# Attention scores of two head pairs in one excursion of the matrix engine, and the values' product in halves around two second layers

## The chip, the cores and the metric

The kernel runs on one core of a Trainium2 chip. The time is that of the whole program on the device, in microseconds. Before the change it is 648.01 us, the median of three runs (647.19 to 648.02).

The core's engines are named as the profile names them: PE multiplies matrices (PEld is its loading of weights), DVE, ACT and POOL work on vectors, SP issues transfers. Each engine takes its instructions from its own queue, in order.

## The reference

Windowed attention over 4 batches, 8 heads, 768 positions and head size 64, with a gated two-layer network behind it (512 to 2048 to 512), all in float32:

```
scores = q @ k.T / sqrt(64) - slope[h] * dist        # 8 global keys, 96 local keys; the rest is masked
a = exp(scores - max);  a = a / (sum(a) + 1e-9)
x = (a @ v), heads side by side: 3072 x 512
h = x @ w_in
out = (h * clip(h + 3, 0, 6) / 6) @ w_out
```

## The kernel before

**Blocks.** The 3072 rows are 8 blocks of 384 rows (three tiles of 128). For the network, the 2048 hidden features are 16 slices of 128. Each slice has a first layer (`first`, L172: 12 matmuls of 384 columns into a PSUM bank of the pool `ps_h`, named hp, which has two banks) and a second layer (`second`, L204: 9 matmuls of 512 columns into the block's three accumulators). Numbers are split in a high and a low part so that two roundings make one float32; that is why each product is three matmuls. Between the layers stands the gate: relu on ACT (L183), a product on DVE (L184), the high part `gh` on POOL (L190) and the low part `gl` on DVE (L197). The tile `g` has one buffer, so the gate of the next slice starts when `gl` is made.

**Slices in pairs.** In the layers of blocks 2 to 7 (`twos`, L490) the slices go in pairs: two first layers, then two steps of other work, then the second layers of the pair before, then two more steps. So a block has 8 slice pairs and the steps 0 to 31: steps 4m and 4m+1 stand behind the first layers of pair m, 4m+2 and 4m+3 behind the second layers that follow them. `attention` (L713) fills these steps with the attention of the next block; each list of functions in `units` is one step.

**A head pair's late attention.** A block has four head pairs (`Pair`, pr 0 to 3, numbered n over all blocks).
- `scale` (L865, POOL) multiplies the queries in their loaded room, in place. There are three rooms; `load_next` (L320) loads pair n + 3 into pair n's room on SP's queue.
- `packed` (L867) makes the scores: 24 small matmuls (48 records in a trace, L879) on parts of the array of 64 rows by 32 columns, into the two banks s and t, one for each head of the pair. `weigh` (L900) then takes each of the three tiles and two heads: a reduction on DVE that also leaves the least value (L908), and the exponential on ACT (L912).
- `sum_up` (DVE) and `normalize` (L932, POOL, two instructions for each tile).
- `spread` (L954, DVE, two transposes for each tile) into the tile `blocks`, whose pool `bp` has one buffer.
- `send` (L960): four transfers on SP's queue copy `blocks` into the pair's rows of `weights_of`.

An interruption of the full-size matmuls of the layers by such small ones is called an excursion here. Before the change the scores of the four pairs stand at the steps 0, 5, 10 and 16 (`TURNS`), and the later functions 3, 4 and 5 steps behind them. The scaling of the next pair's queries stands in the step of the scores.

**The values.** `weighted` (L688) multiplies the four pairs' rows of `weights_of` with the values, on parts of 32 rows by 64 columns, into four banks: one of hp for pair 0, x, t and s for pairs 1, 2 and 3. It stops halfway (`yield`). Its first matmuls read all of `weights_of`. At its end `put_x` (L155) copies each bank into the block's input: high part on ACT (L158), low part on DVE (L159). Before the change the first half runs between the two second layers behind step 25, by the list `between`, and the second half in step 26; the pairs' matmuls of a chunk go in the order 3, 2, 1, 0.

**Order.** `in_order` (L665) keeps the queues of PE, SP and POOL in the order in which the program is written. The order on ACT and DVE is made by a planner that places an instruction where its inputs and buffers are there by its own reckoning.

**The stage before the layers.** `rest_of_third` (L675) attends for the rest of block 2 in the last 8 slices of block 1 and scales the first late pair of block 3. Blocks 3 to 7 attend in the layers of blocks 2 to 6, as described. Block 7's layers hold no attention.

Of the kernel before, what the change touches and what calls it, by code (L numbers as in the profile page):

```python
# [9 lines left out]
F32 = mybir.dt.float32  # L10
# [9 lines left out]
P = 128  # L20
NT = 3
TB = NT * P
NTB = S // TB
NPAIR = H // 2
NKT = DM // P
NF = DF // P
BANK = 512
# [14 lines left out]
PW = PREV + NG + GQ  # L42
# [4 lines left out]
PLAIN = -1 / np.sqrt(D)  # L47
EARLY = 9
ROOMS = 3
TURNS = (0, 5, 10, 16)  # L50
LEAD = 6
WAKE = 9
FIRST = 3
# [10 lines left out]
class Kernel:  # L64
# [425 lines left out]
    def twos(self, steps):  # L490

        for i in range(0, len(steps), 2):
            after = []
            for block, f, x, acc in steps[i:i + 2]:
                g = self.gate(self.first(f, x))
                gh = self.high(g, True)
                after.append((block, f, acc, gh, self.rest(g, gh)))
            yield
            yield
            for self.last in self.pending:  # L500
                self.finish()
                if self.between:
                    self.between.pop()()
            self.pending = after
            yield
            yield
# [30 lines left out]
    def banded(self, flag):  # L537
# [12 lines left out]
        with ExitStack() as early, ExitStack() as words:  # L550
            x0 = self.x_tiles(self.pool("x0", 1, ctx=early, side="right"))
            xs = [x0, self.x_tiles(), self.x_tiles()]
# [8 lines left out]
            with ExitStack() as ctx:  # L561
# [8 lines left out]
                pairs = [Pair(self, n, xs[n // NPAIR], True) for n in range(EARLY)]  # L570
# [6 lines left out]
                for n in range(-2, EARLY + 1):  # L577
# [5 lines left out]
                    if n + 2 < EARLY:  # L583
                        weigh = []
# [46 lines left out]
            for _ in self.halves(todo):  # L631
                pass
            self.decoded_to(2 * NF - 1)
        self.up = self.pool("up", 3, side="right")
        self.bp = self.pool("bp", 1, side="right")
        self.late_tiles()
        self.op = self.pool("op", 3, side="right")
# [1 line left out]
        units, pairs = self.rest_of_third(xs[2], NF - next_f[1])  # L639
# [1 line left out]
            for unit in units[k]:  # L641
                unit()
        self.finish()
        self.pending, self.between = [], []
        self.stage = "layers"
        x, ahead = xs[2], pairs[-1]
        for i in range(2, len(self.blocks)):
            units, x_next = [], None
            if i + 1 < len(self.blocks):
                x_next = self.x_tiles()  # L650
                units, ahead = self.attention(i + 1, x_next, ahead)
            else:
                units = [[]] * 4 + [[lambda: self.doubt(flag)]]
# [7 lines left out]
            x = x_next  # L661
# [13 lines left out]
    def rest_of_third(self, x, slices):  # L675

        units = [[] for _ in range(2 * NF)]
        pairs = [Pair(self, n, x, False) for n in range(EARLY, 3 * NPAIR + 1)]
        pairs[0].scale()
        for p, (me, after) in enumerate(zip(pairs, pairs[1:])):  # L680
            at = units[3 * p + 1:]
            at[0] += [me.packed, after.scale, lambda me=me: self.load_next(me.n, False)]
            at[1] += [me.sum_up] + [lambda t=t, me=me: me.normalize(t) for t in range(NT)]
            at[2] += [lambda t=t, me=me: me.spread(t) for t in range(NT)] + [me.send]
        units[2 * slices - 1].append(lambda: list(self.weighted(pairs[:-1])))
        return units, pairs

    def weighted(self, pairs):  # L688


        nc, block, tb = self.nc, pairs[0].n // NPAIR, pairs[0].tb
        out = {}
        for pair in pairs[::-1]:
            bank = self.bank("xts"[pair.pr - 1]) if pair.pr else self.ps_h.tile([P, BANK], F32, name="hp")
            out[pair.pr] = bank[:, 0:TB]
        groups = self.weights_of.rearrange("p j t g s q -> p j (t g) s q")
        chunks = [(CHUNKS, 0, NT * GROUPS, GROUPS)]
        for c in range(0 if tb else PREV // GQ, CHUNKS):
            chunks.append((c, max(0, c - PREV // GQ), min(NT * GROUPS, c + 1), (c + 1) % GROUPS))
        for n, (c, g0, g1, slot) in enumerate(chunks):  # L700
            if n == len(chunks) // 2:
                yield
            for pr in out:
                own = slice(32 * pr, 32 * pr + 32)
                for j in range(2):
                    nc.tensor.matmul(out[pr][j * D:(j + 1) * D, g0 * GQ:g1 * GQ], lhsT=self.values_of[own, c, j * D:(j + 1) * D],  # L706
                                     rhs=groups[own, j, g0:g1, slot], start=(c == CHUNKS), stop=(c == CHUNKS - 1),
                                     tile_position=(32 * pr, j * D))
        for pr in sorted(out):
            self.put_x(pairs[0].x, pr, out[pr])  # L710
        self.load_values(block + 1)

    def attention(self, i, x, first):  # L713

        units = [[] for _ in range(2 * NF - 2)]
        pairs = [first]
        first.x = x
        for p in range(NPAIR):
            n = i * NPAIR + p
            me, after = pairs[p], Pair(self, n + 1, x, False) if n + 1 < len(self.blocks) * NPAIR else None  # L720
            pairs.append(after)
            at = units[TURNS[p]:]
            at[0] += [me.packed] + [a.scale for a in (after,) if a] + [lambda me=me: self.load_next(me.n, False)]
            at[3] += [me.sum_up, lambda me=me: me.normalize(0), lambda me=me: me.normalize(1)]
            at[4] += [lambda me=me: me.normalize(2), lambda me=me: me.spread(0)]
            at[5] += [lambda me=me: me.spread(1), lambda me=me: me.spread(2), me.send]
        values = self.weighted(pairs[:NPAIR])
        units[25].append(lambda: self.between.append(lambda: next(values)))
        units[26].append(lambda: next(values, None))
        return units, pairs[NPAIR]  # L730


    def general_setup(self):
# [109 lines left out]
class Pair:  # L843
# [20 lines left out]
        _, q = kk.loaded(self.n)  # L864
        nc.gpsimd.tensor_scalar(out=q, in0=q, scalar1=kk.over[:, self.pr:self.pr + 1], scalar2=0.0, op0=ALU.mult, op1=ALU.add)  # L865

    def packed(self):  # L867


        nc, kk = self.nc, self.k  # L870
        self.sums = kk.up.tile([P, 2, 2 * NT], F32, name="sums")
        banks = [kk.bank(b)[:, 0:NT * PW].rearrange("p (t c) -> p t c", t=NT) for b in "st"]
        keys, queries = kk.loaded(self.n)
        for t in range(NT):
            for g in range(GROUPS):
                own, c = slice(g * GQ, (g + 1) * GQ), t * TG + g * GQ
                for j in range(2):
                    rows = slice(j * D, (j + 1) * D)
                    nc.tensor.matmul(banks[j][own, t], lhsT=queries[rows, t, own], rhs=keys[rows, c:c + PW], start=True, stop=True,  # L879
                                     tile_position=(j * D, g * GQ))  # L880
        for t in range(NT):
            self.weigh(t, [bank[:, t] for bank in banks], kk.up.tile([P, 2, PW], F32, name="n"), 0)

    def scores(self, t):
        nc, kk = self.nc, self.k
        if t == 0:
            self.sums = kk.up.tile([P, 2, 2 * NT], F32, name="sums")
        if t != 1:
            self.banks = [kk.bank("s")[:, 0:2 * W].rearrange("p (i c) -> p i c", i=2) for _ in range(2)]
        sp = [self.banks[j][:, t % 2] for j in range(2)]  # L890
        e = kk.up.tile([P, 2, W], F32, name="n")
        lo = self.low(t)
        c = slice(t * TG + lo, t * TG + W)
        keys, queries = kk.loaded(self.n)
        for j in range(2):
            rows = slice(j * D, (j + 1) * D)
            nc.tensor.matmul(sp[j][:, lo:W], lhsT=queries[rows, t], rhs=keys[rows, c], start=True, stop=True)  # L897
        return lambda: self.weigh(t, sp, e, lo)

    def weigh(self, t, sp, e, lo):  # L900
        nc, kk, end = self.nc, self.k, self.end
        for j in range(2):
            h, i = 2 * self.pr + j, 2 * t + j
            if self.plain:
                d, scale = (kk.p0 if lo else kk.p1)[:, h], PLAIN
            else:
                d, scale = kk.dl[:, 0 if self.first(t) else 1], SLOPES[h]
            nc.vector.tensor_tensor_reduce(out=e[:, j, lo:end], in0=sp[j][:, lo:end], in1=d, op0=ALU.add, op1=ALU.min, scale=scale,  # L908
                                           scalar=3.0e38, accum_out=self.least[:, i:i + 1])
        for j in range(2):  # L910
            i = 2 * t + j
            nc.scalar.activation(out=e[:, j, lo:end], in_=e[:, j, lo:end], func=AF.Exp, bias=self.least[:, i:i + 1], scale=-1.0,  # L912
                                 accum_out=self.sums[:, 0, i:i + 1])
        if self.n <= 2:
            kk.held = nc.cur_bb.bb.instructions[-1].name
        self.rows.append(e)

    def sum_up(self, t=None):

# [145 lines left out]
```

## Time and profile before

| | |
|---|---|
| median of three runs | 648.01 us |
| profiled execution, its time | 647.65 us |
| profiled execution, its span | 645.9 us |
| granted PE clock, mean | 0.999 |
| PE busy | 634.3 us (98%) |
| DVE busy | 354.9 us (55%) |
| ACT busy | 255.9 us (40%) |
| POOL busy | 167.4 us (26%) |
| excursions of scores in the layers of blocks 2 to 6 | 20, with 48 records each |

The profile shows one execution. A row of a timeline has the start and the duration in us, the engine, the line of the kernel, the operation, the tile written and those read, the shapes and the count; in square brackets stands how long the engine was idle before it, and what ended that. A row of the chain of waits has start, duration and what ran. Matmuls overlap: a row's duration is longer than the distance to the next row's start, and the distance is what PE's stream takes.

### The profile page before, as it was taken

To read this page: it belongs to the slowest core of one execution; us is meant where nothing else is said; L and a number is where in the kernel's file an instruction comes from. 1 tells how busy PE (TensorE), PEld (TensorE's weight loads), DVE (VectorE), ACT (ScalarE), POOL (GpSimd) and SP (SyncE) were. 2 spreads that over 40 slices of the span, in tenths; PEclk is the share of its full clock that TensorE was granted. 3 is DMA by queue.
4 is the path that set the end of the run, shared out by engine and by line. 5 is a ranking of instruction groups with operands and counts; after the bars stand their busy time and mean duration, and the time that the engine had idled before them with its cause. 6 is when DMAs were issued, how large, how long until landed. Compare 5 with 4: busy or idle time off the path is not lost.

```text
span 645.9 us, 14423 instructions
## 1 busy us (share of the span) xinstructions
PE 634.3 (98%) x5593; PEld 557.5 (86%) x5593; DVE 354.9 (55%) x1066; ACT 255.9 (40%) x706; POOL 167.4 (26%) x371
## 2 busy tenths in 40 slices
PE   9989999999999999999999999999999999999997
PEld 7768999888888888888888888888888888899985
DVE  5889999996645552455534564255623555222222
ACT  5897877775415321242223231143212522221111
POOL 4668000000422441124302332033311242012100
PEclk9999999999999999999999999999999999999999
DMA  7675554543334421242232241223312311110001
GB/s 280 173 227 178 161 159 135 159 135 126 96 73 144 100 79 31 71 123 70 60 98 75 63 102 48 67 79 86 92 31 69 106 33 31 33 50 1 1 1 54
DMA packets 34334, 59.78 MB, mean 93 GB/s; under 512 B 3280, under 2 KB 21200, under 8 KB 33488
## 3 DMA queue, kind: packets, MB, share of 16 engines
q1 hardware_dynamic: 33968, 58.50, 31.4%
q8 instruction: 46, 0.75, 0.5%
q14 instruction: 32, 0.26, 0.1%
q10 hardware_dynamic: 288, 0.26, 0.1%
HBM read 41.16 MB, written 6.29 MB: 73 GB/s over the span
## 4 chain that ended last, share of the span: by engine, by line
PE 89%; DVE 4%; ACT 3%; DMA 1%; POOL 1%; issue 1%; SPq 0%; POOLq 0%; ACTq 0%; DVEq 0%
PE hp L172 40%; PE acc L204 36%; PE sp L879 2%; DVE xl L159 2%; PE sp L204 2%; PE tp L204 1%; PE xp L204 1%; PE sp L706 1%; ACT n L912 1%; DMA wst<-w 1%; POOL n L932 1%; PE tp L706 1%; DMA load<-pairs 1%; PE xp L972 1%; PE sp L897 1%
## 5 line engine op out<-in xcount | busy, mean ns | idle before, releaser
L183 ACT ACTIVATE g<-hp,small 128x384 f32<-128x384 f32 x127 | 73.8, 581 | 261.3 <-PE hp L172 174.5
L172 PE MATMUL hp<-xh,w1h 128*128 128x384 f32 x512 | 174.2, 340 | 0.7 <-DVE xl L159 0.3
L172 PE MATMUL hp<-xh,w1l 128*128 128x384 f32 x512 | 172.4, 337 | 0.1
L172 PE MATMUL hp<-xl,w1h 128*128 128x384 f32 x512 | 171.7, 335 | 0.0
L190 POOL TENSOR_SCALAR gh<-g 128x384 fp32r<-128x384 f32 x104 | 53.5, 515 | 424.4 <-DVE g L184 397.6
L184 DVE SCALAR_TENSOR_TENSOR g<-g,hp 128x384 f32<-128x384 f32 x128 | 70.7, 552 | 122.0 <-ACT g L183 120.7
L204 PE MATMUL acc<-w2h,gh 128*128 128x512 f32 x336 | 133.2, 396 | 0.0
L204 PE MATMUL acc<-w2h,gl 128*128 128x512 f32 x336 | 131.9, 393 | 0.0
L204 PE MATMUL acc<-w2l,gh 128*128 128x512 f32 x336 | 131.7, 392 | 0.0
L197 DVE TENSOR_TENSOR gl<-g,gh 128x384 fp32r<-128x384 f32 x128 | 71.4, 558 | 66.4 <-POOL gh L190 59.0
L172 PEld LDWEIGHTS hp<-xh,w1h 128*128 128x128 f32 x512 | 96.1, 188 | 7.0 <-DVE xl L159 2.3
L912 ACT ACTIVATE n<-n,least 128x136 f32<-128x136 f32 (+2 forms) x192 | 79.9, 418 | 54.2 <-DVE least L908 53.4
L172 PEld LDWEIGHTS hp<-xl,w1h 128*128 128x128 f32 x512 | 96.1, 188 | 2.6
L172 PEld LDWEIGHTS hp<-xh,w1l 128*128 128x128 f32 x512 | 96.1, 188 | 0.9 <-DVE w1l L439 0.8
L932 POOL TENSOR_SCALAR n<-n,sums 128x136 f32<-128x136 f32 (+2 forms) x186 | 82.4, 460 | 39.7 <-DVE sums L923 23.8
L204 PEld LDWEIGHTS acc<-w2h,gh 128*128 128x128 f32 x336 | 63.1, 188 | 15.4 <-issue 3.8
L204 PEld LDWEIGHTS acc<-w2h,gl 128*128 128x128 f32 x336 | 63.0, 188 | 13.8 <-DVE gl L197 0.3
L204 PEld LDWEIGHTS acc<-w2l,gh 128*128 128x128 f32 x336 | 63.1, 188 | 11.3
L954 DVE STREAM_TRANSPOSE blocks<-n 128x256 f32<-128x256 f32 x138 | 51.2, 424 | 22.8 <-POOL n L932 21.4
L912 ACT ACTIVATION_READ_ACCUMULATOR n<-n,least 128x1 f32 x192 | 36.3, 189 | 0.0
L399 ACT ACTIVATE wz<-wst 128x512 f32<-128x512 f32 x32 | 21.6, 679 | 5.7 <-DVE w2l L439 3.9
L446 DVE CUSTOM_DVE_ANT_0 wz<-wz,we 128x1024 uint16<-128x1024 uint16 x32 | 22.2, 695 | 1.3 <-POOL we L404 0.9
(126 smaller groups left out, 728.6 us busy)
## 6 DMA issues: line engine op xcount, KB each, us to landing
wst<-w SPq DMA_DIRECT2D x32, 512.0 KB, 3.6
load<-pairs SPq DMA_DIRECT2D x31, 444.0 KB, 3.5
weights<-blocks SPq DMA_DIRECT2D x92, 120.0 KB, 2.4
values<-values SPq DMA_DIRECT2D x6, 1024.0 KB, 5.4
out<-o SPq DMA_DIRECT2D x23, 256.0 KB, 2.4
values<-pairs SPq DMA_DIRECT2D x9, 384.0 KB, 3.6
out<-o ACTq DMA_DIRECT2D x1, 256.0 KB, 3.0
load<-pairs SPq DMA_DIRECT2D x1, 252.0 KB
```

The lines of the kernel that those rows point to most:

```text
L159: nc.vector.tensor_tensor(out=xl[:, pair, :], in0=ps, in1=xh[:, pair, :].bitcast(F32), op=ALU.subtract)
L172: self.nc.tensor.matmul(hp, lhsT=self.w1(w, f)[:, kt, :], rhs=a[:, kt, :], start=(n == 0), stop=(n == 3 * NKT - 1))
L183: nc.scalar.activation(out=g, in_=hp, func=AF.Relu, bias=self.three, scale=1.0)
L184: nc.vector.scalar_tensor_tensor(out=g, in0=g, scalar=6.0, in1=hp, op0=ALU.min, op1=ALU.mult)
L190: self.nc.gpsimd.tensor_scalar(out=gh, in0=g, scalar1=1.0, scalar2=0.0, op0=ALU.mult, op1=ALU.add)
L197: self.nc.vector.tensor_tensor(out=gl, in0=g, in1=gh.bitcast(F32), op=ALU.subtract)
L204: self.nc.tensor.matmul(acc[tt], lhsT=a[:, tk], rhs=self.w2(w, f), start=(f == 0 and j == 0), stop=(f == NF - 1 and j == 2))
L399: self.nc.scalar.activation(out=self.z[i].bitcast(F32), in_=words[:, :, 1].bitcast(F32), func=AF.Abs)
L446: tt(out=z, in0=z, in1=self.e.pop(i), op=ALU.add)
L912: nc.scalar.activation(out=e[:, j, lo:end], in_=e[:, j, lo:end], func=AF.Exp, bias=self.least[:, i:i + 1], scale=-1.0, accum_out=self.sums ...
L932: nc.gpsimd.tensor_scalar(out=e[:, j, lo:end], in0=e[:, j, lo:end], scalar1=over, scalar2=0.0, op0=ALU.mult, op1=ALU.add)
L954: nc.vector.transpose(out=self.blocks[:, :, t, 4 * s:4 * s + 4], in_=e[:, :, c:c + P].rearrange("p j (b q) -> p j b q", b=4))
```

## The change

- The scores of two pairs of a block stand in one step, at the steps 2 and 14 (`TURNS`). The first pair of such a couple writes one bank of hp and the bank x, the second s and t. For the first pair, head 0 is weighed over all tiles before head 1.
- In a couple, the first pair's `sum_up`, `normalize`, `spread` and `send` stand 3, 4 and 5 steps behind the scores, the second pair's 5, 6 and 7.
- The queries of the next couple's first pair are scaled in the step of the scores, those of its second pair 5 steps later. In the stage before the layers, the second late pair of block 3 is scaled too.
- The pool `up`, which holds the scores' tiles, has 6 buffers instead of 3.
- The first half of the values runs in step 25, ahead of both second layers, the second half in step 26 as before; `between` is gone. The pairs' matmuls of a chunk go in the order 0, 1, 2, 3.

The diff, cut to its core:

```
-TURNS = (0, 5, 10, 16)
+TURNS = (2, 14)
...
                 self.finish()
-                if self.between:
-                    self.between.pop()()
...
-        self.up = self.pool("up", 3, side="right")
+        self.up = self.pool("up", 6, side="right")
...
-        x, ahead = xs[2], pairs[-1]
+        x, ahead = xs[2], pairs[-2:]
...
     def rest_of_third(self, x, slices):
-        pairs = [Pair(self, n, x, False) for n in range(EARLY, 3 * NPAIR + 1)]
+        pairs = [Pair(self, n, x, False) for n in range(EARLY, 3 * NPAIR + 2)]
         pairs[0].scale()
-        for p, (me, after) in enumerate(zip(pairs, pairs[1:])):
+        for p, (me, after) in enumerate(zip(pairs[:-2], pairs[1:])):
...
-        units[2 * slices - 1].append(lambda: list(self.weighted(pairs[:-1])))
+        at[4].append(pairs[-1].scale)
+        units[2 * slices - 1].append(lambda: list(self.weighted(pairs[:-2])))
...
     def weighted(self, pairs):
-        for pair in pairs[::-1]:
+        for pair in pairs:
...
-    def attention(self, i, x, first):
+    def attention(self, i, x, pairs):
         units = [[] for _ in range(2 * NF - 2)]
-        pairs = [first]
-        first.x = x
-        for p in range(NPAIR):
-            n = i * NPAIR + p
-            me, after = pairs[p], Pair(self, n + 1, x, False) if n + 1 < len(self.blocks) * NPAIR else None
-            pairs.append(after)
-            at = units[TURNS[p]:]
-            at[0] += [me.packed] + [a.scale for a in (after,) if a] + [lambda me=me: self.load_next(me.n, False)]
-            at[3] += [me.sum_up, lambda me=me: me.normalize(0), lambda me=me: me.normalize(1)]
-            at[4] += [lambda me=me: me.normalize(2), lambda me=me: me.spread(0)]
-            at[5] += [lambda me=me: me.spread(1), lambda me=me: me.spread(2), me.send]
+        for pair in pairs:
+            pair.x = x
+        pairs = pairs + [Pair(self, n, x, False) for n in range(i * NPAIR + 2, min(i * NPAIR + 6, len(self.blocks) * NPAIR))]
+        for p in range(0, NPAIR, 2):
+            couple, after = pairs[p:p + 2], pairs[p + 2:p + 4]
+            at = units[TURNS[p // 2]:]
+            at[0] += [lambda me=me, first=first: me.packed(first) for me, first in zip(couple, (True, False))]
+            at[0] += [a.scale for a in after[:1]] + [lambda me=me: self.load_next(me.n, False) for me in couple]
+            at[5] += [a.scale for a in after[1:]]
+            for k, me in enumerate(couple):
+                at[2 * k + 3] += [me.sum_up, lambda me=me: me.normalize(0), lambda me=me: me.normalize(1)]
+                at[2 * k + 4] += [lambda me=me: me.normalize(2), lambda me=me: me.spread(0)]
+                at[2 * k + 5] += [lambda me=me: me.spread(1), lambda me=me: me.spread(2), me.send]
         values = self.weighted(pairs[:NPAIR])
-        units[25].append(lambda: self.between.append(lambda: next(values)))
-        units[26].append(lambda: next(values, None))
-        return units, pairs[NPAIR]
+        for k in (25, 26):
+            units[k].append(lambda: next(values, None))
+        return units, pairs[NPAIR:]
...
-    def packed(self):
+    def packed(self, first=False):
-        banks = [kk.bank(b)[:, 0:NT * PW].rearrange("p (t c) -> p t c", t=NT) for b in "st"]
+        banks = [kk.ps_h.tile([P, BANK], F32, name="hp"), kk.bank("x")] if first else [kk.bank("s"), kk.bank("t")]
+        banks = [bank[:, 0:NT * PW].rearrange("p (t c) -> p t c", t=NT) for bank in banks]
...
-        for t in range(NT):
-            self.weigh(t, [bank[:, t] for bank in banks], kk.up.tile([P, 2, PW], F32, name="n"), 0)
+        self.rows = [kk.up.tile([P, 2, PW], F32, name="n") for _ in range(NT)]
+        for heads in ((0,), (1,)) if first else ((0, 1),):
+            for t in range(NT):
+                self.weigh(t, [bank[:, t] for bank in banks], self.rows[t], 0, heads)
...
-    def weigh(self, t, sp, e, lo):
+    def weigh(self, t, sp, e, lo, heads=(0, 1)):
-        for j in range(2):
+        for j in heads:
```

More of the change, by code (lines that the diff above doesn't have):

```diff
@@ L643, in banded @@
         self.finish()
-        self.pending, self.between = [], []
+        self.pending = []
         self.stage = "layers"
-        x, ahead = xs[2], pairs[-1]
+        x, ahead = xs[2], pairs[-2:]
         for i in range(2, len(self.blocks)):
@@ L897, in scores @@
             nc.tensor.matmul(sp[j][:, lo:W], lhsT=queries[rows, t], rhs=keys[rows, c], start=True, stop=True)
+        self.rows.append(e)
         return lambda: self.weigh(t, sp, e, lo)
-    def weigh(self, t, sp, e, lo):
+    def weigh(self, t, sp, e, lo, heads=(0, 1)):
         nc, kk, end = self.nc, self.k, self.end
-        for j in range(2):
+        for j in heads:
             h, i = 2 * self.pr + j, 2 * t + j
@@ L909, in weigh @@
                                            scalar=3.0e38, accum_out=self.least[:, i:i + 1])
-        for j in range(2):
+        for j in heads:
             i = 2 * t + j
@@ L915, in weigh @@
             kk.held = nc.cur_bb.bb.instructions[-1].name
-        self.rows.append(e)
     def sum_up(self, t=None):
```

## The prediction

> **What bounds the kernel now.** I read the page's shares first, then its chain of work that ended last, then the waits of the matrix engine, and last the timelines of single excursions and of the engines around them.
>
> ```profile
> PE 634.3 (98%) x5593; PEld 557.5 (86%) x5593; DVE 354.9 (55%) x1066; ACT 255.9 (40%) x706; POOL 167.4 (26%) x371
> ...
> PEclk9999999999999999999999999999999999999999
> ...
> PE 89%; DVE 4%; ACT 3%; DMA 1%; POOL 1%; issue 1%; SPq 0%; POOLq 0%; ACTq 0%; DVEq 0%
> ...
> PE hp L172 <- DVE xl L159: 0.3, 2, 0.2
> ```
>
> PE is busy 98% of the span and holds 89% of the chain; in the layers it hardly waits. A change gains by what it takes out of PE's queue and loses by any wait that it puts there. The other engines count only where their work comes late for PE.
>
> One excursion of scores, in PE's timeline (start, duration):
>
> ```profile
> 294.48 0.39 PE L204 MATMUL acc<-w2l,gh 128*128 128x512 f32 x1
> 294.70 0.39 PE L204 MATMUL acc<-w2h,gl 128*128 128x512 f32 x1
> 295.02 0.30 PE L879 MATMUL sp<-load 64*32 64x136 f32 x1
> ...
> 295.16 0.28 PE L879 MATMUL sp<-load 64*32 64x136 f32 x1
> ...
> 295.62 0.28 PE L879 MATMUL sp<-load 64*32 64x136 f32 x1
> ...
> 295.92 0.45 PE L172 MATMUL hp<-xh,w1h 128*128 128x384 f32 x1
> 296.20 0.34 PE L172 MATMUL hp<-xl,w1h 128*128 128x384 f32 x1
> 296.38 0.33 PE L172 MATMUL hp<-xh,w1l 128*128 128x384 f32 x1
> ```
>
> Full matmuls start 0.23 us (second layer) and 0.175 us (first layer) apart. From 294.70 to 296.20 are 1.50 us; less one spacing of each kind, an excursion costs **1.10 us**. Its 48 records go in groups of eight, (295.62 - 295.16) / 4 = 0.115 us apart, so the scores take 6 x 0.115 = 0.69 us and going out and back costs **0.41 us**.
>
> **The change part by part.**
>
> **Couples.** Blocks 3 to 7 attend during blocks 2 to 6. In these 5 blocks four excursions become two; the matmuls stay. That takes out 10 x 0.41 = **4.1 us**. Not shown before is a change of banks inside an excursion: at best it costs nothing; at worst what the way out costs, 295.02 - 294.70 - 0.23 = 0.09 us each, 0.9 us in all. I take nothing, since banks s and t have been read long before.
>
> The first pair's scores take one of the two hp banks. The next-but-one first layer needs it back about 2.2 us after the excursion; three reductions of 0.22 us free it, and DVE is empty by then (the earlier transposes are two slice pairs back). Without that cover it would cost what six transposes hold DVE, 2.20 us less the slack, about nothing. Loads go two at a time through SP's queue, each behind its pair's scores; nothing of that block stands behind them until the next sends some 12 us later. The queries' scaling is 0.59 us of POOL, five steps later than its load.
>
> **Order of the values' pairs.** After the second half of the values, x is copied in this order (ACT, DVE, PE):
>
> ```profile
> 259.02 0.48 ACT L158 CAST xh<-sp 128x384 fp32r<-128x384 f32 x1 [7.37 <-PE tp L706]
> ...
> 260.14 0.51 ACT L158 CAST xh<-hp 128x384 fp32r<-128x384 f32 x1
> ```
>
> ```profile
> 260.94 0.55 DVE L159 TENSOR_TENSOR xl<-hp,xh 128x384 fp32r<-128x384 f32 x1
> ```
>
> ```profile
> 261.06 0.34 PE L172 MATMUL hp<-xh,w1l 128*128 128x384 f32 x1
> 261.54 0.44 PE L172 MATMUL hp<-xh,w1h 128*128 128x384 f32 x1
> 261.82 0.34 PE L172 MATMUL hp<-xl,w1h 128*128 128x384 f32 x1
> ```
>
> The hp bank is copied last, at 261.49, and PE's next first layer waits for it: 261.82 - 261.06 - 2 x 0.175 = 0.41 us, in each of the 5 blocks. The change writes pair 0 (hp) first in each chunk, and the copies followed the order of the banks' last matmuls, so hp should be copied first and free by about 260.1: **2.1 us** less. The bounds are 0 and 2.1; I take 2.1.
>
> **First half of the values before both second layers.** Its own cost on PE is the same at either boundary, but it now comes 2.09 us earlier, and it reads what the last pair sends. Before, in the chain of waits, with the send from SP's timeline:
>
> ```profile
> 313.86 4.18 PE hp L172 x24
> 318.04 4.12 PE acc L204 x18
> 322.17 4.18 PE hp L172 x24
> 326.35 2.09 PE acc L204 x9
> 328.44 0.47 PE sp L706 x2
> ...
> 330.44 2.27 PE acc L204 x9
> ```
>
> ```profile
> 322.33 2.56 SPq L960 DMA_DIRECT2D weights<-blocks  x4
> ```
>
> How long a send takes shows where the next pair's transposes had to wait for the single buffer "blocks":
>
> ```profile
> 167.59 2.69 SPq L960 DMA_DIRECT2D weights<-blocks  x4
> ```
>
> ```profile
> 172.19 0.77 DVE L954 STREAM_TRANSPOSE blocks<-n 128x256 f32<-128x256 f32 x2 [1.44 <-DMA weights<-blocks]
> ```
>
> That is 4.60 us with 2.69 us of issue, so 4.45 us with the usual 2.55. The send of 322.33 is there at 326.78: 1.7 us ahead of PE's 328.44, but 0.4 us after 326.35, where the change reads it. Even if nothing else moved, PE would wait **0.4 us** a block.
>
> More moves. The couple's second pair normalizes in the same three steps as the old fourth pair (19 to 21 of the slices' steps), but its first pair now does so two steps ahead of it instead of six or more. How late that runs, the old excursion at step 10 shows, which also stands ahead of first layers (zero = 295.92; ACT, POOL, DVE, SP):
>
> ```profile
> 297.00 0.41 ACT L912 ACTIVATE n<-n,least 128x136 f32<-128x136 f32 x1 [4.94 <-DVE least L908]
> ...
> 299.38 0.57 ACT L183 ACTIVATE g<-hp,small 128x384 f32<-128x384 f32 x1
> ```
>
> ```profile
> 303.24 0.51 POOL L190 TENSOR_SCALAR gh<-g 128x384 fp32r<-128x384 f32 x1 [2.02 <-DVE g L184]
> 303.73 2.56 POOL L932 TENSOR_SCALAR n<-n,sums 128x136 f32<-128x136 f32 x6
> ```
>
> ```profile
> 304.90 2.20 DVE L954 STREAM_TRANSPOSE blocks<-n 128x256 f32<-128x256 f32 x6 [0.56 <-POOL n L932]
> ```
>
> ```profile
> 307.13 2.54 SPq L960 DMA_DIRECT2D weights<-blocks  x4
> ```
>
> Six exponentials take 299.38 - 297.00 = 2.38 us (0.397 each), and the gate's relu comes right behind all six, though its first layer had ended at about 298.1. POOL's queue is in order, so the normalizations stand behind that slice pair's gh; the send starts at +11.21.
>
> After: scores start 0.90 + 0.69 = 1.59 us before zero; the first reduction follows 1.0 us after an excursion's start on an idle DVE:
>
> ```profile
> L879 PE MATMUL acc<-load x144: 276/276/301, 158.2 to 173.6; 64*32 64x136 f32 x144
> ```
>
> ```profile
> 159.23 0.30 DVE L908 CUSTOM_DVE_ANT_0 n<-acc,dl 128x136 f32<-128x136 f32 x1 [0.61 <-PE acc L879]
> ```
>
> The first exponential follows 0.37 us later, at -0.2. If the relu again stands behind all of them, now twelve, it runs at -0.2 + 12 x 0.397 = +4.57 instead of +3.46, and the first pair's send at 11.21 + 1.11 = +12.3. It lands 4.45 us later, at +16.8; only then may the second pair's six transposes start.
>
> POOL meanwhile: six normalizations to 306.29 - 295.92 + 1.11 = +11.5, the moved scaling (0.59), four of the second pair (1.45) to +13.5, and only then the next slices' gh:
>
> ```profile
> 317.33 0.51 POOL L190 TENSOR_SCALAR gh<-g 128x384 fp32r<-128x384 f32 x1 [2.15 <-DVE g L184]
> 319.86 0.51 POOL L190 TENSOR_SCALAR gh<-g 128x384 fp32r<-128x384 f32 x1 [2.02 <-DVE g L184]
> 320.35 1.14 POOL L932 TENSOR_SCALAR n<-n,sums 128x136 f32<-128x136 f32 x2
> ```
>
> From the first gh to the last normalization's end these rows have 4.16 us: +17.7. The transposes go from +16.8 to about +19.0, the send follows and lands at +23.5. PE reaches the first half at 4.18 + 0.1 + 4.12 + 4.18 + 4.12 + 4.18 = +20.9. The wait is **2.6 us** a block, 13.0 us in all. Its lower bound is the 0.4 us above (2 us in all). The upper bound comes from DVE's order. A gate's product stands 0.72 us ahead of its gh:
>
> ```profile
> 319.14 0.55 DVE L184 SCALAR_TENSOR_TENSOR g<-g,hp 128x384 f32<-128x384 f32 x1 [0.71 <-ACT g L183]
> ```
>
> The later slice's product is due at 13.5 + 2.53 - 0.72 = +15.3. If it stands behind the first waiting transposes, it runs at 16.8 + 0.7 = +17.5, its gh at +18.2, the last normalizations end at +19.8, and the send of +20.6 lands at +25.0: a wait of 4.1 us. If the earlier slice's gl is the one behind them (due at +14.1), the same steps start 1.3 us later: 5.4 us. Behind PE's wait stand the second layers and everything after them; nothing hides it.
>
> **Sum.** The profiled execution took 647.65 us (span 645.9), 0.36 below the median of the three. 647.65 - 4.1 - 2.1 + 13.0 = **654.5 us**.
>
> **The clock.** The profile's clock row is 9 in all 40 slices, and PE has no rest of microseconds in the layers that could lower it; the sum leaves it so. [...]
>
> **The rivals.**
>
> (1) *The gates pass the exponentials* (ends on the other side). Where ACT's planned order runs the relu when its layer ends, at about +2.2, the send starts some 10.0 us after zero, lands at +14.5, no longer holds the transposes, and the wait shrinks to its bound: 647.65 - 6.2 + 2.1 = 643.6 us. For it: that order is not written in the kernel. Against: in the rows above the relu stood behind every ready exponential. It decides at a wait of 6.2 / 5 = 1.24 us, a relu at about +3.2, behind eight or nine of the twelve.
>
> (2) *A transpose blocks the gates.* Waits of 4.1 to 5.4 us: 662 to 668.5 us. For it: row 172.19, where the gate's step came after the waiting transposes. Against: with a landing at +16.8 the gate's steps are mostly ready earlier.
>
> (3) *PE is slow after its rest*, on top of (2). If PE came out of the wait at half pace for the first half of the values alone (330.44 - 328.44 = 2.0 us), it would lose 2.0 x 5 = 10 us more: about 672 us. Against: the clock row, though no rest of that length stands in it. [...]
>
> (4) *The copies keep their order*, hp last: 2.1 us given back, 656.6 us with the wait, 645.7 with rival (1).
>
> **How the numbers follow.** Forecast (wait of 1.9 to 3.3 us, 651 to 658 us): 0.42; with hp last too (4): 0.05. Rival (1), 643 to 646: 0.23. In between, the relu behind 8 to 10 exponentials, a wait of 1 to 1.8 us, 646.5 to 650.5 us: 0.14, of it 0.07 within 0.2%, 0.05 above, 0.02 below. Rival (2) 0.13, with (3) 0.03. The range 642.5 to 662 leaves out most of (2) and (3); the forecast's own is 650 to 658.5. A measurement of this kernel tells about 0.2% (1.3 us) from no change. Faster 0.25, same 0.07, slower 0.68: 0.42 + 0.05 + 0.05 + 0.16 are the last.
>
> **What would show it.** Right: 10 groups of 96 score records in the layers, each about 1.8 us on PE; in 5 places PE idle for 2 to 3 us at L706 behind the first seconds of a half, released by the sends; the fourth pair's send some 19 us after its couple's excursion; the relu behind twelve exponentials; hp's copy first and no gap at the first layer after it. Wrong: the relu among the exponentials, and L706 waiting under 1 us; then the time is 643 to 646. Also wrong: PE waiting at L172 for the reductions of the hp bank, which I cost at nothing.

## The result, and the profile after

The changed kernel takes 665.85 us (median of four runs, 664.31 to 667.55), the kernel before 647.60 us (four runs, 647.04 to 648.02). The ratio is 1.0279 [1.0266, 1.0292]: 18.2 us slower. The prediction had 654.5 us: the right sign, and some 11 us too little. The profiled execution took 664.31 us, with a span of 662.5 us and a mean granted clock of 0.987.

The page of the changed kernel, and the row of the waits of the matrix engine (total us, times, longest) that is new:

```profile
PE 640.9 (97%) x5593; PEld 565.8 (85%) x5593; DVE 352.4 (53%) x1066; ACT 254.7 (38%) x706; POOL 168.7 (25%) x371
...
PEclk9999999999999999999999998999999999799999
...
PE 79%; DVE 6%; DMA 5%; SPq 2%; ACT 2%; POOL 2%; issue 2%; DVEq 0%; POOLq 0%; ACTq 0%
```

```profile
PE sp L705 <- DMA weights<-blocks: 11.0, 5, 2.7
```

PE runs the same 5593 matmuls and is busy 6.6 us *longer*, although two excursions a block are gone. It now waits five times for a send, and the clock row has an 8 and a 7. The chain that ended last has given ten points from PE to the sends and to what feeds them. So there are two losses: a wait, and matmuls that take longer.

**The wait.** The chain of work up to it, in the first of the five blocks, by engine. First PE's timeline around the couple's second excursion:

```profile
227.12 0.39 PE L204 MATMUL acc<-w2h,gl 128*128 128x512 f32 x1
...
228.85 0.28 PE L881 MATMUL tp<-load 64*32 64x136 f32 x1
229.06 0.44 PE L172 MATMUL hp<-xh,w1h 128*128 128x384 f32 x1
229.34 0.34 PE L172 MATMUL hp<-xl,w1h 128*128 128x384 f32 x1
```

From 227.12 to 229.34, less a spacing of each kind (0.23 and 0.175), are 1.81 us for 96 records, where two excursions of 48 took 2 x 1.10. Zero is 229.06. Then ACT's timeline, DVE's and SP's:

```profile
228.80 0.41 ACT L917 ACTIVATE n<-n,least 128x136 f32<-128x136 f32 x1 [3.51 <-DVE least L913]
...
233.53 0.56 ACT L183 ACTIVATE g<-hp,small 128x384 f32<-128x384 f32 x1
...
261.20 0.48 ACT L158 CAST xh<-hp 128x384 fp32r<-128x384 f32 x1 [9.98 <-PE xp L705]
```

```profile
245.83 1.42 DVE L958 STREAM_TRANSPOSE blocks<-n 128x256 f32<-128x256 f32 x4 [1.02 <-DMA weights<-blocks]
```

```profile
241.32 2.63 SPq L964 DMA_DIRECT2D weights<-blocks  x4
```

```profile
248.41 2.55 SPq L964 DMA_DIRECT2D weights<-blocks  x4
```

The relu stands behind all twelve exponentials, at +4.5 (times with a plus are counted from zero; the last ACT row shows hp as the first bank copied); the first pair's send starts at +12.3 and lands at +16.8, where DVE's transposes were held; the second pair's send follows at +19.4. PE meets it here, in all five blocks (start of the first half, then the fourth pair's first matmul, with PE's idle time before it in brackets):

```profile
250.06 0.54 PE L705 MATMUL hp<-weights,values 32*64 32x384 f32 x2
...
252.83 0.54 PE L705 MATMUL sp<-weights,values 32*64 32x384 f32 x2 [1.88 <-DMA weights<-blocks]
...
255.03 0.50 PE L204 MATMUL acc<-w2h,gh 128*128 128x512 f32 x1
...
327.35 0.54 PE L705 MATMUL hp<-weights,values 32*64 32x384 f32 x2
...
330.17 0.54 PE L705 MATMUL sp<-weights,values 32*64 32x384 f32 x2 [1.93 <-DMA weights<-blocks]
...
405.75 0.54 PE L705 MATMUL hp<-weights,values 32*64 32x384 f32 x2
...
409.21 0.59 PE L705 MATMUL sp<-weights,values 32*64 32x384 f32 x2 [2.57 <-DMA weights<-blocks]
...
486.77 0.54 PE L705 MATMUL hp<-weights,values 32*64 32x384 f32 x2
...
489.54 0.54 PE L705 MATMUL sp<-weights,values 32*64 32x384 f32 x2 [1.88 <-DMA weights<-blocks]
...
563.49 0.54 PE L705 MATMUL hp<-weights,values 32*64 32x384 f32 x2
...
567.21 0.90 PE L705 MATMUL sp<-weights,values 32*64 32x384 f32 x2 [2.73 <-DMA weights<-blocks]
```

The other three pairs' first matmuls run, then PE rests. The same half before the change, between the second layers of that block:

```profile
252.57 0.54 PE L706 MATMUL sp<-weights,values 32*64 32x384 f32 x2
...
254.91 0.50 PE L204 MATMUL acc<-w2h,gh 128*128 128x512 f32 x1
```

It took 254.91 - 252.57 = 2.34 us, and now 255.03 - 250.06 = 4.97: 2.63 us more. From the half's start to the fourth pair's first matmul are 2.77 us there, so 0.14 us of this is work that runs anyway. The other blocks have 2.82, 3.46, 2.77 and 3.72; less 0.14 each, the five waits are 2.63, 2.68, 3.32, 2.63 and 3.58: **14.8 us**.

**The slow matmuls.** Stretches of PE's time (length; busy time of PE, PEld, DVE, ACT, POOL; then the granted clock, the DMA share and GB/s):

```profile
252.83:255.03 2.20, 2.20 (x116) 1.87 (x117) 0.00 (x0) 0.00 (x0) 0.00 (x0) 1.00 0.00 0
330.17:332.95 2.78, 2.78 (x85) 2.29 (x85) 0.00 (x0) 0.00 (x0) 0.00 (x0) 0.66 0.02 6
331.07:334.48 3.41, 3.41 (x60) 2.79 (x57) 0.00 (x0) 0.00 (x0) 0.00 (x0) 0.50 0.02 5
409.21:412.82 3.61, 3.61 (x116) 2.94 (x117) 0.00 (x0) 0.00 (x0) 0.00 (x0) 0.55 0.02 5
409.57:416.40 6.83, 6.83 (x112) 5.39 (x97) 0.00 (x0) 0.00 (x0) 0.00 (x0) 0.50 0.01 2
489.54:491.42 1.88, 1.88 (x85) 1.55 (x85) 0.00 (x0) 0.00 (x0) 0.00 (x0) 1.00 0.00 0
566.59:573.41 6.82, 6.20 (x121) 4.99 (x122) 0.00 (x0) 0.00 (x0) 0.00 (x0) 0.50 0.02 4
567.21:571.17 3.96, 3.96 (x116) 3.13 (x116) 0.00 (x0) 0.00 (x0) 0.00 (x0) 0.50 0.02 4
```

The 116 records of the half behind the wait take 2.20 us in the first block at full clock, 3.61 us in the third at 0.55 and 3.96 us in the fifth at 0.50. The 85 records take 2.78 us in the second and 1.88 us in the fourth. The second layers behind it are slow too, in PE's timeline of the third block:

```profile
413.41 0.63 PE L204 MATMUL acc<-w2l,gh 128*128 128x512 f32 x1
413.84 0.63 PE L204 MATMUL acc<-w2h,gl 128*128 128x512 f32 x1
```

They start 0.43 us apart instead of 0.23. The clock stood at 0.50 for 3.41 us in the second block, 6.83 us in the third and 6.82 us in the fifth, where PE was at work for 6.20 us of it. If all of that work goes at half pace, half of the time is lost: (3.41 + 6.83 + 6.20) / 2 = **8.2 us**. That is an upper estimate, since the small matmuls of the fifth block took 1.8 times their 2.20 us and not twice. The first and fourth blocks lose nothing. With the sum of the prediction's kind: 647.65 - 10 x (2 x 1.10 - 1.81) - 2.1 + 14.8 + 8.2 = 664.7 us, against 664.31 measured.

### The profile page after: what moved, and what is told of

Same layout as the page of the kernel before. It is cut to its first block, busy times and chain, and to the rows that moved or that the text cites. A ratio compares the mean times of both kernels' runs of the same rounds, so it can differ in the third digit from the quotient of the medians.

```text
span 662.5 us, 14378 instructions
## 1 busy us (share of the span) xinstructions
PE 640.9 (97%) x5593; PEld 565.8 (85%) x5593; DVE 352.4 (53%) x1066; ACT 254.7 (38%) x706; POOL 168.7 (25%) x371
## 4 chain that ended last, share of the span: by engine, by line
PE 79%; DVE 6%; DMA 5%; SPq 2%; ACT 2%; POOL 2%; issue 2%; DVEq 0%; POOLq 0%; ACTq 0%
PE hp L172 34%; PE acc L204 32%; DMA weights<-blocks 4%; DVE blocks L958 3%; SPq L964 2%; POOL n L936 2%; PE sp L204 2%; PE sp L705 1%; PE tp L204 1%; PE xp L204 1%; ACT n L917 1%; PE hp L705 1%; PE hp L881 1%; DMA wst<-w 1%; DVE g L184 1%
## 5 line engine op out<-in xcount | busy, mean ns | idle before, releaser
L172 PE MATMUL hp<-xh,w1h 128*128 128x384 f32 x512 | 174.1, 340 | 0.1
L172 PE MATMUL hp<-xh,w1l 128*128 128x384 f32 x512 | 172.4, 337 | 0.1
L172 PE MATMUL hp<-xl,w1h 128*128 128x384 f32 x512 | 171.8, 336 | 0.0
L204 PE MATMUL acc<-w2l,gh 128*128 128x512 f32 x336 | 133.1, 396 | 0.0
L172 PEld LDWEIGHTS hp<-xh,w1h 128*128 128x128 f32 x512 | 96.1, 188 | 5.6 <-DVE least L913 1.9
L172 PEld LDWEIGHTS hp<-xl,w1h 128*128 128x128 f32 x512 | 96.1, 188 | 2.5
L172 PEld LDWEIGHTS hp<-xh,w1l 128*128 128x128 f32 x512 | 96.1, 188 | 0.9 <-DVE w1l L439 0.8
L936 POOL TENSOR_SCALAR n<-n,sums 128x136 f32<-128x136 f32 (+2 forms) x186 | 80.5, 450 | 17.7 <-DVE sums L927 12.5
L705 PE MATMUL sp<-weights,values 32*64 32x128 f32 (+4 forms) x296 | 23.7, 315 | 11.0 <-DMA weights<-blocks 11.0
L705 PEld LDWEIGHTS sp<-weights,values 32*64 32x64 f32 x296 | 18.6, 152 | 15.5 <-DMA weights<-blocks 10.8
```

Source lines behind the costliest of these rows:

```text
L172: self.nc.tensor.matmul(hp, lhsT=self.w1(w, f)[:, kt, :], rhs=a[:, kt, :], start=(n == 0), stop=(n == 3 * NKT - 1))
L204: self.nc.tensor.matmul(acc[tt], lhsT=a[:, tk], rhs=self.w2(w, f), start=(f == 0 and j == 0), stop=(f == NF - 1 and j == 2))
L936: nc.gpsimd.tensor_scalar(out=e[:, j, lo:end], in0=e[:, j, lo:end], scalar1=over, scalar2=0.0, op0=ALU.mult, op1=ALU.add)
```

## The experiments

All are compared with the kernel before on the same chip, in runs of their own: 647.19 us (19 runs) for the first four, 647.13 us (17 runs) for the others. So what a run wins or loses is taken as its distance from its own runs of the kernel before; the changed kernel's is 18.2 us. The theory: the time is lost to the wait for the last send, in its length and in the clock after it, and the couples themselves save what was forecast. The main rival: the couples themselves cost time.

### Couples kept, the first half back between the second layers

```
             for self.last in self.pending:
                 self.finish()
+                if self.between:
+                    self.between.pop()()
...
-        for k in (25, 26):
-            units[k].append(lambda: next(values, None))
+        units[25].append(lambda: self.between.append(lambda: next(values)))
+        units[26].append(lambda: next(values, None))
```

> The couples are kept, the first half of the values goes back between the two second layers. Theory A (the lost time is PE's wait for the last send of a block, plus the slower clock that follows such a wait): the last send lands about 23.8 us after the couple's excursion, PE reaches the half at 20.9 + 2.1 = 23.0 us, so 0.8 us of waiting a block is left and no slow clock: 647.6 - 4.1 - 2.1 + 4 = about 645.5 us. Rival B (the couples themselves cost the time, by the hp bank or by twelve exponentials ahead of the gates): the time stays above 655 us.

Measured: 649.14 us (646.86 to 651.71), ratio 1.0028 [1.0011, 1.0045]. Some 16.3 us of the 18.2 are gone with this one part undone, so the rival falls. But the time is 3.6 us above the expectation: about 2 us a block of delay doesn't fully cover a wait of 2.6 to 3.6. By the reckoning above, waits of 0.55 to 2.4 us are left, 6.0 us in all where 4 were expected. And one block of the profiled execution (651.71 us) shows the whole pattern again, PE's timeline first, then the stretch at half clock:

```profile
556.23 0.90 PE L707 MATMUL sp<-weights,values 32*64 32x384 f32 x2 [1.66 <-DMA weights<-blocks]
```

```profile
556.24:563.06 6.82, 6.82 (x123) 5.43 (x124) 0.00 (x0) 0.00 (x0) 0.00 (x0) 0.50 0.01 2
```

After an idle stretch of only 1.66 us the clock fell to 0.50 for 6.82 us, which is worth up to 3.4 us. That a block may or may not fall goes with the scatter of 4.8 us over the ten runs: the four slowest (650.65 to 651.71 us) have a mean clock of 0.994, the lowest, and the other six 0.995 to 1.000.

### The same waits, with PE kept at work

Twelve matmuls of 128 x 128 that compute nothing needed are put into the bank s ahead of each first half; the values overwrite them.

```
+        if self.stage == "layers":
+            any_ = self.three.broadcast_to([P, P])
+            for _ in range(12):
+                nc.tensor.matmul(out[3][:, 0:P], lhsT=any_, rhs=any_, start=True, stop=True)
         for n, (c, g0, g1, slot) in enumerate(chunks):
```

> As the changed kernel, with 12 idle matmuls of 128 x 128 ahead of each first half of the values, about 2.6 us in which PE would wait anyway; their result is overwritten. Theory A: the wait is unchanged in length but PE does not rest, so the clock stays full: 647.6 - 6.2 + 13 to 15 = 654.5 to 656.5 us, and the clock row has 9 everywhere. Rival B or one by which the waits alone are the loss (the slow clock costs nothing): 664 to 667 us as the changed kernel, or more by the idle matmuls.

Measured: 657.23 us (655.82 to 657.57), ratio 1.0146 [1.0129, 1.0163], and a clock of 1.000. PE's timeline and the stretch:

```profile
250.08 2.84 PE L702 MATMUL sp<-small 128*128 128x128 f32 x24
...
253.18 0.54 PE L709 MATMUL sp<-weights,values 32*64 32x384 f32 x2
```

```profile
249.90:252.90 3.00, 3.00 (x32) 2.88 (x31) 1.11 (x2) 0.58 (x1) 0.68 (x2) 1.00 0.80 164
```

The filler removes the rest, not the wait: the fourth pair starts at 253.18, even 0.35 us later than in the changed kernel. Still, it is 10.0 us behind the kernel before instead of 18.2, so 8.2 us faster, as the stretches gave. So work that does nothing makes the program faster, because the matmuls behind it run at full clock. This is the experiment that settles the second loss. It came out 0.7 us above its expectation; from PE's reaching the half to the fourth pair's first matmul, the five blocks have 16.5 us here and 15.5 in the changed kernel, which covers that. With these 0.9 us of longer delay the clock's part in the medians is some 9 us; the profiled execution of the changed kernel, with its 8.2, was the fastest of four.

### The values in one piece behind both second layers

```
-        for k in (25, 26):
-            units[k].append(lambda: next(values, None))
+        units[26].append(lambda: list(values))
```

> Both halves of the values in one excursion behind both second layers. Theory A: PE reaches the values at 20.9 + 4.1 = 25.0 us after the couple's excursion, the last send lands at 23.8: no wait, no slow clock, and one excursion a block less (0.41 us each): 647.6 - 4.1 - 2.1 - 2.1 = 639.3 us. Rival B: above 655 us.

Measured: 647.07 us (645.85 to 650.24), ratio 1.0002 [0.9988, 1.0015]: no wait for a send and a full clock, but nearly 8 us above the expectation. Two of the five places, in PE's timeline:

```profile
258.76 0.24 PE L705 MATMUL hp<-weights,values 32*64 32x96 f32 x1 [1.16 <-issue]
...
334.45 0.27 PE L705 MATMUL sp<-weights,values 32*64 32x64 f32 x2 [1.43 <-issue]
```

In every block PE pauses once for 1.2 to 1.4 us in the middle of the small matmuls, after some 190 to 220 records of the uninterrupted run. "issue" says that no instruction or transfer of the kernel held it. Five pauses are 6.4 us, most of the miss. In the halves (half the matmuls, at most 128 records in the traces of both kernels) there is none. What PE waits for is not shown. By the trace's DMA records one 16 KB packet moves near it in each of the five blocks, on the queue that the page names "instruction" (q8): it starts 1.2 to 1.4 us before the pause does, and PE goes on 2.4 to 2.7 us after that start. Whether the two are connected no run tests. So the result doesn't show what the halves alone are worth, except that here splitting pays for itself.

### The second pair weighed two steps later in the program

The reductions and exponentials of a couple's second pair are written behind the next first layers, so that the planner may place the relu between the two pairs' exponentials.

```
-            at[0] += [lambda me=me, first=first: me.packed(first) for me, first in zip(couple, (True, False))]
+            at[0] += [lambda me=me, first=first: me.packed(first, not first) for me, first in zip(couple, (True, False))]
+            at[2].append(lambda me=couple[1]: me.late())
```

> As the changed kernel, but the second pair of a couple is weighed two steps later, behind the next first layers, so that the gates' relu stands behind six exponentials instead of twelve. Theory A: the chain to the last send is shorter by about 2.2 us and bounded by the gates: the wait falls to 0.4 to 1 us a block and the clock stays full: 643.5 to 647 us. Rival C (the chain is held by the single buffer of the transposes, not by the order on ACT): a wait of over 2 us stays and the time is above 652 us.

Measured: 667.92 us (665.98 to 669.17), ratio 1.0318 [1.0293, 1.0342]. ACT's timeline:

```profile
229.09 0.41 ACT L922 ACTIVATE n<-n,least 128x136 f32<-128x136 f32 x1 [3.49 <-DVE least L918]
...
233.81 0.56 ACT L183 ACTIVATE g<-hp,small 128x384 f32<-128x384 f32 x1
```

The relu still stands behind twelve exponentials: the place in the program did not move ACT's order. So the run is no test of the order. It is another look at the clock, though: here it fell behind all five waits, whose idle stretches were 1.91 to 2.66 us (granted clock 0.79 from 252 to 260 us, 0.83 from 330 to 340 and from 410 to 420, 0.54 from 490.54 to 498, 0.86 from 568 to 580).

### The gates ahead of the second pair's exponentials

As the run before, but each of the second pair's exponentials is also ordered behind the last relu written before it.

```
+            if behind:
+                kk.tc.add_manual_dep(nc.cur_bb.bb.instructions[-1], kk.gated, ...)
```

> As the changed kernel, with the second pair's exponentials made to stand behind the next relu in ACT's order; the edit before this one left ACT's order as it was. Theory A: the relu runs at about +2.3 us instead of +4.5, the chain to the last send is shorter by some 2 us, the wait falls to 0.4 to 1 us a block, no slow clock: 643.5 to 647 us. Rival C (the chain is held by the single buffer of the transposes, whatever ACT does): a wait of over 2 us stays, above 652 us.

Measured: 648.01 us (647.40 to 649.02), ratio 1.0012 [1.0003, 1.0021]. ACT, SP and PE:

```profile
231.03 0.58 ACT L183 ACTIVATE g<-hp,small 128x384 f32<-128x384 f32 x1 [0.26 <-PE hp L172]
```

```profile
238.87 2.56 SPq L973 DMA_DIRECT2D weights<-blocks  x4
```

```profile
251.54 0.54 PE L706 MATMUL sp<-weights,values 32*64 32x384 f32 x2 [1.09 <-DMA weights<-blocks]
```

Now the order is the one that the rival (1) of the prediction needed. The relu comes 2.5 us earlier, and so does the first send (238.87 against 241.32). The waits, by the same reckoning as above, shrink to 0.66 to 2.1 us, 6.1 us in all, the clock stays at 0.999, and 17.4 us come back. But it is 1.0 us above the expectation, and 4.4 us above that rival's 643.6: the first send now took 5.66 us until the transposes behind it could start (at 244.53 by DVE's timeline), not 4.45, so the second send came only 1.3 us earlier. The single buffer, rival C of this run, still holds part of the chain. The two long waits, 1.8 and 2.1 us in the first and third blocks, are those where a 16 KB packet of the queue q8 moved during the first send; the other three are 0.66 to 0.81 us.

### The move alone, on the kernel before

```
-        units[25].append(lambda: self.between.append(lambda: next(values)))
+        units[25].append(lambda: next(values))
```

> The kernel before with one edit: the first half of the values ahead of both second layers. Theory A: the last send, whose chain is as before, lands 0.4 us after PE gets there: about 0.4 us a block, no slow clock, 649 us (same to slower by 0.3%). Rival D (the move of the values alone is what costs the time): over 655 us.

Measured: 650.88 us (650.54 to 651.53), ratio 1.0053 [1.0039, 1.0067]. PE:

```profile
251.20 0.54 PE L706 MATMUL sp<-weights,values 32*64 32x384 f32 x2 [0.48 <-PE hp L172]
```

Without any couple the move costs 3.75 / 5 = 0.75 us a block. That is above the expectation of 0.4 us, which is also the prediction's lower bound for the wait. These waits, with 0.46 to 0.55 us of idle time ahead of the half, brought no slower clock: 0.999 in the profiled execution.

### The values' order alone, on the kernel before

```
-        for pair in pairs[::-1]:
+        for pair in pairs:
```

> The kernel before with one edit: the pairs' matmuls of a chunk in the order 0, 1, 2, 3. Theory A: the hp bank is copied first, the gap of 0.41 us at the next first layer goes in each of 5 blocks: 647.2 - 2.1 = 645.1 us. Rival: the copies keep their order or the gap goes elsewhere: 647.2 us.

Measured: 645.43 us (644.34 to 646.51), ratio 0.9969 [0.9958, 0.9981], 1.7 us faster (1.2 to 2.7 by the interval). ACT's timeline:

```profile
259.27 0.48 ACT L158 CAST xh<-hp 128x384 fp32r<-128x384 f32 x1 [7.39 <-PE xp L706]
```

The copies follow the order of the pairs, hp first; the gap of 0.41 us at the next first layer is gone.

### The second couple two steps earlier

```
-TURNS = (2, 14)
+TURNS = (2, 12)
```

> As the changed kernel with the second couple at step 12 instead of 14. Theory A: the chain to the last send starts 4.1 us earlier and lands before PE gets to the first half: no wait, no slow clock, 647.2 - 4.1 - 2.1 = 641.0 us. Rival B (the couples themselves cost time): above 650 us.

Measured: 641.40 us (641.13 to 641.60), ratio 0.9909 [0.9894, 0.9924]. SP's timeline and PE's:

```profile
243.83 2.56 SPq L964 DMA_DIRECT2D weights<-blocks  x4
```

```profile
249.46 0.54 PE L705 MATMUL hp<-weights,values 32*64 32x384 f32 x2
...
249.50 0.54 PE L705 MATMUL sp<-weights,values 32*64 32x384 f32 x2
```

The last send starts 5.6 us ahead of the half that reads it, the fourth pair's matmuls follow the first pair's by 0.04 us, and the clock is 1.000. With the same couples, order and halves it is 5.7 us faster than the kernel before and 24.0 us faster than the changed one: what lay between is the wait and its clock. Less the 1.7 us of the order alone, the couples give 4.0 us. This version beats both kernels, and its four runs lie within 0.5 us; those of the changed kernel spread over 3.2 us.

## Why the prediction was right and wrong

- **Couples, 4.1 us.** Right: an excursion of 96 records takes 1.81 us, so 0.39 a couple by the trace, 3.9 us in all; 4.0 us by the runs. The change of banks inside cost nothing to speak of: 1.81 us against the 1.10 + 0.69 = 1.79 of one excursion and a second pair's scores.
- **The hp bank as cover, at nothing.** Right: no row of PE's waits in the changed kernel has a first layer (L172) waiting for a reduction.
- **The order of the values' pairs, 2.1 us.** Right in mechanism; alone it measured 1.7 us, with 2.1 inside its interval.
- **The path to the last send.** Right at every station of the first block, within 0.3 us: relu +4.5 (forecast +4.57), first send +12.3 (+12.3), its landing +16.8 (+16.8), PE at the half +21.0 (+20.9), the last landing +23.8 (+23.5).
- **The wait, 2.6 us a block and 13.0 us in all.** Right in three blocks (2.63 to 2.68) and in its cause. In the third and fifth it was 3.3 and 3.6 us, 14.8 us in all. The forecast took one block for all five. It is not rival (2): in DVE's timeline the transposes of these two blocks start

```profile
402.14 1.43 DVE L958 STREAM_TRANSPOSE blocks<-n 128x256 f32<-128x256 f32 x4 [1.59 <-DMA weights<-blocks]
...
560.12 0.77 DVE L958 STREAM_TRANSPOSE blocks<-n 128x256 f32<-128x256 f32 x2 [2.36 <-DMA weights<-blocks]
```

  behind a first send that was issued at 397.05 and 554.79: it took 5.09 and 5.33 us to land instead of 4.51 in the first block (its issue alone 3.13 and 3.27 us instead of 2.63). That is 0.6 and 0.8 us of the 0.7 and 0.9 us by which these waits are longer. By the trace's DMA records, a 16 KB packet of the queue q8 ("instruction") moved in the middle of both sends, from 398.20 and from 556.78; in the first block's send such a packet moved at the very start, from 241.36 to 242.24, and none moved during the sends of the second and fourth, which took 4.49 and 4.45 us to land. The term of the sum that was mis-sized here is the landing of 4.45 us, taken as the same everywhere.
- **The clock, at zero.** Here the forecast failed: "the sum leaves it so". The sum was made with a full clock because every slice before showed one; but no slice before held a rest of that length, as rival (3) says itself: PE's longest wait in the layers before is 0.2 us. The stretches put the loss at 8.2 us, the run with filled waits at 8 to 9. In the runs, of the idle stretches from 1.66 us (in the first experiment) up to 2.73 us all were followed by a clock of 0.50 but two, of 1.88 us. And rival (3), which had the right mechanism (PE slow after its rest), was tied to rival (2) and given 0.03. Its half pace was the author's estimate, shown by no row before; the small matmuls of the third and fifth blocks took 3.61 and 3.96 us instead of 2.20. Standing by itself on the forecast's wait that rival would have been 654.5 + 10 = 664.5 us, near the 665.85 measured. Part of that is luck: the 10 us were 2.0 us at half pace in all five blocks, and the trace has 3.41 to 6.83 us at half clock in three.
- **The range, 642.5 to 662.** Missed by 3.9 us at its upper end, because a rest of 2.6 us was forecast with 0.42 and its effect on the clock had hardly a chance of its own.
- **Rival (1), 643.6 us.** Its order did not come by itself, and when forced gave 648.0: the relu's place decides 8.8 of the 14.8 us of waits and, with them, the clock, but the first send took longer when it started earlier, which the sum had not.

What decides between a fall of the clock and none at nearly equal rests? By the clock records of the changed kernel's trace the clock changes at 331.07, 334.48, 409.57, 416.40, 566.59 and 573.41 us: these lie 1, 22, 2, 44 and 2 times 3.413 us apart. Cut from 331.07 us into stretches of that length, the trace gives a grid. Three of its stretches hold the fuller part of the first, second and fourth rest (the row's first figures are the length and PE's busy time, the 1.00 is the clock):

```profile
249.15:252.56 3.41, 1.80 (x18) 0.88 (x16) 1.22 (x3) 0.58 (x1) 1.03 (x2) 1.00 0.71 144
327.65:331.07 3.42, 1.49 (x46) 0.77 (x36) 0.75 (x2) 0.58 (x1) 0.51 (x1) 1.00 0.54 108
488.08:491.49 3.41, 1.95 (x85) 1.66 (x85) 0.45 (x1) 0.00 (x0) 0.51 (x1) 1.00 0.25 50
```

The rest of 1.93 us lay whole in one such stretch, and the clock fell at the stretch's end, at 331.07. So it did at 409.57 and 566.59, behind stretches with 2.57 and 2.12 us of idle time, in the third and fifth blocks. The two rests of 1.88 us lay across an edge, with 1.61 and 1.46 us of idle time in the fuller stretch, and the clock stayed at 1.00. The other traces, cut along their own grids, say the same: in the layers, every stretch with 1.66 us or more of idle PE was followed by half clock for one stretch or two, and none with 1.46 us or less; in between, one with 1.54 us, in the run with the second pair weighed two steps later, was and the one with 1.61 us was not. So in these runs the fall went with the idle time within one stretch of 3.413 us, and with where a rest lay against the grid. No run varies that alone, and why a fall lasts one stretch or two stays open.

## What to carry to other kernels

Price a wait of the matrix engine as its length and as what the matmuls behind it lose if they start at half clock: here nine of the eleven idle stretches of 1.66 to 2.73 us were followed by a clock of 0.50, and 14.8 us of waits brought some 8 us more. Before moving a reader of transferred data earlier, lay out the last writer's path station by station, and move the writer by more than the slack that is missing: two steps of the schedule made 2.8% slower into 0.9% faster. If a wait can't be removed, giving the engine idle work during it can be worth more than the work costs: here 8.2 us net.

## What the runs showed of the hardware that was not expected

- The granted clock fell to 0.50 for 3.41 or 6.83 us behind rests of 1.66 to 2.73 us, in three of five places in one execution (the changed kernel), in five of five in another (the second pair weighed two steps later) and in one in a third (the first half back between the second layers). The changes of the clock in the changed kernel's trace lie 1, 22, 2, 44 and 2 times 3.413 us apart.
- PE pauses 1.2 to 1.4 us after 190 to 220 records of an uninterrupted run of small matmuls, held by no instruction or transfer of the kernel, in five of five blocks; the halves, runs of at most 128 records, show none. A 16 KB packet of the queue "instruction" starts shortly before each pause; that it is the cause is not shown.
- Four transfers of the same tile took about 4.5 us from the first issue to the landing in one place (241.32 to 245.83), 5.09 and 5.33 us in two others, where the issue was longer by 0.5 and 0.6 us, and 5.66 us in another kernel, with an issue of 2.56 us. During each of the three long ones a 16 KB packet of the queue "instruction" moved, and one also moved at the start of the send of 241.32; whether it lengthens a send no run shows.
